# A short convolution of four taps spread over four 32-row tiles of the array, and a program put in line anew

## The chip, the cores and the metric

The kernel runs on one core of a Trainium2 chip. The metric is device time in microseconds (us) of one launch. Five engines work side by side and meet through semaphores: PE (TensorE, matmuls; its weight loads are listed apart as PEld), DVE (VectorE), ACT (ScalarE), POOL (GpSimd) and SP (SyncE), whose queue issues most of the transfers.

## The reference

All inputs are bf16. S = 2048 positions, D = 640 channels, F = 1728.

```python
x = A_q
h  = x + A(layernorm(x), k, v, shift_k, ssm_k, ssm_D)
h2 = h + B(layernorm(h))

def A(q, k, v, shift_k, ssm_k, ssm_D):
    # short causal convolution along the positions, each channel by itself
    k_pad = pad(k, 3 zero rows in front)
    k_shift = sum(k_pad[t:t + S, :] * shift_k[:, 3 - t] for t in range(4))
    kv = k_shift * v
    # long causal convolution of kv with ssm_k, by transforms over 2*S points
    y = irfft(rfft(pad(kv)) * rfft(pad(ssm_k)))[:S] + kv * ssm_D
    return q * y

def B(x):
    return (silu(x @ w_gate) * (x @ w_up)) @ w_down
```

## The kernel before

The 2048 positions go in four blocks of 512 (`BLK`); inside a block position 4p + r lies in partition p, row r (r = 0 to 3). For every block j the kernel

- loads k, turns it (channels to partitions) into `kT` and does the short convolution: for each r and each group c of 128 channels four matmuls add up in PSUM, with a slice of `kT` as weights and a 128x128 diagonal of tap weights (`diag`) streamed through. That is 4 x 5 x 4 = 80 pairs of weight load and matmul in a block (`kv_of`, line 540). The sum is multiplied by v into `kv` (tile t): in block 0 by DVE straight out of PSUM (line 545), in the others after a copy by ACT (line 547) by DVE (line 548), once for each r;
- transforms `kv` and the filter block `g` into spectra (`spectrum`, PE line 345, taken out of PSUM by ACT line 334 or DVE line 337), called X and G;
- multiplies and adds the spectra of all block pairs up to j on DVE (`mac`, lines 560, 582, 587, 588). Block 3 has the most of these;
- goes back by `inverse` (PE line 703), multiplies by the normed input, adds it to x (DVE lines 717, 723), norms the rows again and turns them into `hT` (`turn_h`, PE line 743 or a transposing transfer);
- runs the feed-forward part (`ffn`): gate and up products (PE lines 789 and 824), silu and product (ACT 807 and 813, DVE 815), down product with `wd` (PE line 856), output.

PSUM is eight banks, held as two pairs `ps_c` and two pairs `ps_f`. The conv side takes `ps_c` (in block 0 it takes `ps_f` and `ps_c` in turn, `conv_ps`), the feed-forward side takes `ps_f`.

The order of the work is made when the program is built. `Plan` holds every step with an engine, an assumed length, what it reads and writes and a priority; the priority of a stage is a due time plus the number that the table `PLACE` gives under the stage's name (Lk1 is the load of k of block 1, G2 the spectrum of filter block 2, m02 a product of spectra, i3 an inverse, f1 a feed-forward part). `schedule` then lists the steps one by one, and each engine gets its instructions in that order. So the table sets only the order in which instructions stand on each engine; on the chip each starts when those ahead of it on its engine are done and its semaphores are there.

The feed-forward part of block j stands beside the conv side of block j + 1, and that of block 3 stands alone at the end.

Of the kernel before, what the change touches and what calls it, by code (L numbers as in the profile page):

```python
# [11 lines left out]
BF16 = mybir.dt.bfloat16  # L12
# [14 lines left out]
KT = D // P  # L27
NC_FULL = 13
# [4 lines left out]
PAD = 16  # L33
DIRECT, ACTLN, ACTKV, ACTLN2 = ('inv0', 'G0', 'G1'), 1, 1, (2, 3)
# [5 lines left out]
PLACE = {"G0": 26.0, "G1": -15.5, "G2": -8.0, "G3": 12.0, "LWF": -13.5, "LWI": 16.0, "Ld": 20.0, "Lg0": -24.0,  # L40
# [47 lines left out]
class Plan:  # L88
# [4 lines left out]
    def __init__(self, slots, in_turn=()):  # L93
        self.ops, self.slots = [], slots
        self.turn = {t: [] for t in in_turn}
        self.at = {}
        self.all = 0.0

    def line(self, block, name, at, **own):

        at += PLACE.get(name, 0.0)
        self.block, self.all, self.at = block, at, {e: p + PLACE.get(name + e, 0.0) for e, p in own.items()}

    def add(self, eng, ns, fn, reads=(), writes=(), holds=(), other=None):
# [12 lines left out]
        op.other = other  # L117
        for acc, is_w in [(a, False) for a in reads] + [(a, True) for a in writes]:
            b, part = acc if isinstance(acc, tuple) else (acc, None)
            b.log.append((op, part, is_w))  # L120
# [5 lines left out]
    def schedule(self):  # L126
# [10 lines left out]
        while todo:  # L137
            found = []
            for op in todo:
                ready = 0.0  # L140
# [27 lines left out]
            assert best is not None, "the plan is stuck"  # L168
# [36 lines left out]
def kernel(ctx: ExitStack, tc: tile.TileContext, A_q, A_k, A_v, A_shift_k, A_ssm_k, A_ssm_D, B_x,  # L205
# [83 lines left out]
    diag = fixed([P, KT * 4, P], BF16, "diag")  # L289
# [212 lines left out]
    def load_k(j):  # L502

        kT = new("kT")
        if j == 0:
            load(MB, lambda: nc.sync.dma_start(out=plain(kT), in_=block(kk, j)), [kT])
        for r in range(R) if j else ():
            plan.add("turn", MB / 4 / 300.0, lambda r=r: nc.sync.dma_start(
                out=ap(kT)[:, :, r, PAD:], in_=block(kk, j)[:, r, :], transpose=True), [], [(kT, r)])
        return kT  # L510

    def turned_k(k):
        kT = new("kT")
        for r in range(R):
# [5 lines left out]
            pe(290, tr, [k, ident], [pt], [kT])  # L520
# [4 lines left out]
    def kv_of(j, kT, before, v):  # L525
# [7 lines left out]
        for r in range(R):  # L533
            ps = conv_ps()

            def mm(r=r, ps=ps):
                for c in range(KT):
                    for t in range(4):
                        q, off = (r - t, PAD) if r >= t else (r - t + 4, PAD - 1)
                        nc.tensor.matmul(line(ap(ps))[:, c * P:(c + 1) * P], ap(kT)[:, c, q, off:off + P],  # L540
                                         ap(diag)[:, 4 * c + t, :], start=(t == 0), stop=(t == 3))
            pe(1130, mm, [kT, diag], [ps], [kv])

            def straight(r=r, ps=ps):
                nc.vector.tensor_mul(ap(kv)[:, r, :], line(ap(ps)), rd(v)[:, r, :])
            if plan.block >= ACTKV:
                op = plan.add("act", 700, lambda r=r, ps=ps: nc.scalar.copy(ap(kv)[:, r, :], line(ap(ps))), [ps, v], [(kv, r)], (), ("dve", 820, straight))
                op.rest = dve(490, lambda r=r: nc.vector.tensor_mul(ap(kv)[:, r, :], ap(kv)[:, r, :], rd(v)[:, r, :]), [v], [(kv, r)])
            else:
                dve(820, straight, [ps, v], [(kv, r)])  # L550
        return kv

    def mac(A, X, H, first, pieces=((0, 1),), adds=()):
# [23 lines left out]
        for xs, hs, dst, f in ((0, 0, 0, nc.vector.tensor_add), (0, 1, 1, nc.vector.tensor_add),  # L577
# [3 lines left out]
            if (xs, hs) in adds:  # L581
                dve(1490, lambda b=b, xs=xs, hs=hs: nc.vector.tensor_mul(flat2(b), X.part(xs), H.part(hs)), [X.at(xs), H.at(hs)], [b], [A.b])
                add_into(lambda dst=dst: A.part(dst), lambda b=b: flat2(b), [b], [A.at(dst)])
                continue
# [164 lines left out]
    def load_w(gi):  # L749
        w = new("wgu")  # L750
        was = plan.all
        if plan.block == 0 and gi < 2:
            plan.all = PLACE.get("Lwg", 5.0)
        f0 = gi * 2 * P
# [10 lines left out]
        plan.all = was  # L765
# [116 lines left out]
    load(1e3, lambda: nc.sync.dma_start(out=ap(tapw), in_=A_shift_k.rearrange("(c p) t -> p c t", p=P)), [tapw])  # L882
# [3 lines left out]
    def blank():  # L886
# [3 lines left out]
    plan.add("pool", 2000, blank, [], [blanks])  # L890
    k = load_k(0)
    dve(2800, lambda: nc.vector.tensor_mul(
        ap(diag), ap(ident).unsqueeze(1).to_broadcast([P, KT * 4, P]),
        ap(tapw).rearrange("p c t -> p (c t)").unsqueeze(2).to_broadcast([P, KT * 4, P])), [ident, tapw], [diag])
# [130 lines left out]
```

## Time and profile before

| | us |
|---|---|
| median of 3 runs | 282.18 (281.87 to 284.87) |
| the profiled execution | 282.56 |
| its span, first to last instruction | 280.8 |
| PE busy | 260.9 (93%) |
| DVE busy | 207.0 (74%) |
| ACT busy | 175.6 (63%) |
| short convolution, PE matmuls of line 540 | 320 pairs |

Outside the span of the profiled execution lie 1.76 us. Busy times count each instruction from its start to its modelled end; matmuls overlap their neighbours, so what PE needs is read from how far apart starts lie, not from the mean length of one. The granted TensorE clock is 1.0 throughout.

### The profile page before, as it was taken

How to read it: one execution, taken by the hardware profiler on the slowest of the kernel's cores; microseconds unless marked ns; L12 is line 12 of the kernel's file. 1: busy time of each engine (PE TensorE's matmuls, PEld its weight loads, DVE VectorE, ACT ScalarE, POOL GpSimd, SP SyncE). 2: the span in 40 equal slices, each digit the busy share in tenths (PEclk: the TensorE clock that was granted, in tenths of full speed). 3: DMA queues.
4: the chain of work that ended last, by engine and by line, in shares of the span. 5: the costliest groups of instructions: out<-in, count | busy, mean ns of one | idle time of the engine just before them, and what ended most of it. 6: DMA issues, size and time to landing. Idle time of an engine off the chain costs nothing.

```text
span 280.8 us, 4663 instructions
## 1 busy us (share of the span) xinstructions
PE 260.9 (93%) x1787; PEld 162.0 (58%) x1804; DVE 207.0 (74%) x294; ACT 175.6 (63%) x285; POOL 52.8 (19%) x71
## 2 busy tenths in 40 slices
PE   0699989899999999999999999998989999999994
PEld 0686766645456677965545567643435774444672
DVE  0568996988999988899998999999999630011211
ACT  5547746998896877487756886386348643454300
POOL 2030100000398001131003101234950121000000
PEclk9999999999999999999999999999999999999999
DMA  7999992289957734959557495859545244653011
GB/s 251 338 366 237 240 233 98 93 194 250 258 118 92 216 122 101 170 83 205 143 141 150 98 245 85 174 117 232 148 102 152 27 47 86 170 154 59 0 49 48
DMA packets 74553, 42.77 MB, mean 152 GB/s; under 512 B 34145, under 2 KB 71842, under 8 KB 74530
## 3 DMA queue, kind: packets, MB, share of 16 engines
q1 hardware_dynamic: 71410, 37.88, 53.2%
q0 software_dynamic: 3120, 4.59, 11.6%
q8 instruction: 14, 0.23, 0.3%
q14 instruction: 9, 0.07, 0.1%
HBM read 30.01 MB, written 4.59 MB: 123 GB/s over the span
## 4 chain that ended last, share of the span: by engine, by line
PE 68%; DVE 16%; DMA 6%; ACT 6%; issue 2%; SPq 0%; DVEq 0%; ACTq 0%
PE ps_f L789 26%; PE ps_f L856 16%; PE ps_c L345 8%; PE ps_c L703 6%; DVE scr L587 5%; DVE S L588 5%; PE ps_c L540 5%; PE ps_f L824 4%; DMA kT<-in_A_k_dram 2%; DMA ld<-in_A_ssm_k_dram 2%; DMA wgu<-in_B_w_gate_dram 2%; ACT S L334 2%; DVE S L560 1%; PE ps_f L540 1%; ACT sg L807 1%
## 5 line engine op out<-in xcount | busy, mean ns | idle before, releaser
L789 PE MATMUL ps_f<-hT,wgu 128*128 128x512 bf16 x465 | 106.6, 379 | 3.3 <-ACT sg L807 2.3
L789 PEld LDWEIGHTS <-wgu 128*128 128x128 bf16 x480 | 46.7, 98 | 56.2 <-issue 2.8
L856 PE MATMUL ps_f<-wd,tT 128*128 128x320 bf16 x448 | 63.5, 299 | 0.1
L856 PEld LDWEIGHTS <-tT 128*128 128x128 bf16 x448 | 43.7, 98 | 17.2 <-issue 0.4
L807 ACT ACTIVATE sg<-ps_f 128x1024 bf16<-128x1024 f32 (+1 forms) x28 | 27.0, 963 | 24.6 <-PE ps_f L789 12.5
L815 DVE TENSOR_TENSOR tT<-sg,sg 128x1024 bf16<-128x1024 bf16 (+1 forms) x27 | 17.5, 647 | 27.4 <-ACT sg L813 27.4
L345 PE MATMUL ps_c<-t,WF 128*128 128x320 bf16 x208 | 34.9, 299 | 0.6 <-ACT S L334 0.5
L813 ACT CAST sg<-ps_f 128x1024 bf16<-128x1024 f32 (+1 forms) x27 | 25.6, 950 | 14.5 <-PE ps_f L789 14.5
L588 DVE TENSOR_TENSOR S<-S,scr 128x2560 bf16<-128x2560 bf16 x21 | 31.4, 1493 | 0.7
L587 DVE TENSOR_TENSOR scr<-S,S 128x2560 bf16<-128x2560 bf16 x21 | 31.2, 1485 | 0.3 <-DMA S<-scr 0.2
L345 PEld LDWEIGHTS <-WF 128*128 128x128 bf16 x240 | 23.4, 98 | 13.2 <-issue 1.5
L598 ACT ACTIVATE row<-x 128x640 bf16<-128x640 bf16 x32 | 23.4, 733 | 5.5 <-DVE x L723 5.1
L862 POOL DMA_DIRECT2D out_dram<-o x12 | 10.6, 883 | 70.7 <-ACT o L861 70.7
L334 ACT CAST S<-ps_c 128x640 bf16<-128x640 f32 (+1 forms) x31 | 18.9, 622 | 7.0 <-PE ps_c L345 6.4
L540 PEld LDWEIGHTS <-kT 128*128 128x128 bf16 x320 | 20.1, 103 | 2.3 <-issue 0.8
L540 PE MATMUL ps_c<-diag,kT 128*128 128x128 bf16 x280 | 17.7, 223 | 0.7 <-DVE hT L745 0.7
L648 ACT ACTIVATE row<-x,sm 128x640 bf16<-128x640 bf16 x17 | 15.0, 919 | 2.7 <-DMA x<-row 1.3
L637 ACT ACTIVATE row<-x 128x640 bf16<-128x640 bf16 x16 | 11.7, 731 | 7.5 <-DMA x<-in_A_q_dram 7.5
L703 PEld LDWEIGHTS <-WI 128*128 128x128 bf16 x128 | 12.4, 98 | 6.8 <-issue 1.2
L861 ACT CAST o<-ps_f 128x640 bf16<-128x640 f32 x12 | 8.2, 687 | 10.8 <-PE ps_f L856 10.8
L717 DVE SCALAR_TENSOR_TENSOR row<-row,ps_c 128x640 bf16<-128x640 bf16 x14 | 11.5, 819 | 3.7 <-PE ps_c L703 3.6
L824 PE MATMUL ps_f<-hT,wgu 128*128 128x512 bf16 x58 | 13.8, 379 | 0.1
(105 smaller groups left out, 293.6 us busy)
## 6 DMA issues: line engine op xcount, KB each, us to landing
wgu<-in_B_w_gate_dram SPq DMA_DIRECT2D x24, 320.0 KB, 3.5
wgu<-in_B_w_up_dram SPq DMA_DIRECT2D x24, 320.0 KB, 3.6
x<-in_A_q_dram SPq DMA_DIRECT2D x4, 640.0 KB, 3.8
ld<-in_A_v_dram SPq DMA_DIRECT2D x4, 640.0 KB, 5.8
ld<-in_A_ssm_k_dram SPq DMA_DIRECT2D x4, 640.0 KB, 5.3
wd<-in_B_w_down_dram SPq DMA_DIRECT2D x1, 2080.0 KB, 12.0
out_dram<-x SPq DMA_DIRECT2D x3, 640.0 KB, 3.6
out_dram<-o POOLq DMA_DIRECT2D x12, 160.0 KB, 3.5
```

The lines of the kernel that those rows point to most:

```text
L334: (lambda: nc.scalar.activation(dst(), src(), ACT.Copy, scale=2.0)) if twice else (lambda: nc.scalar.copy(dst(), src())),
L345: nc.tensor.matmul(ap(ps)[:, h, 0:NH], w, ap(src)[:, r, h * NH:(h + 1) * NH], start=(first and i == 0), stop=(last and i == len(rs) - 1), ...
L540: nc.tensor.matmul(line(ap(ps))[:, c * P:(c + 1) * P], ap(kT)[:, c, q, off:off + P], ap(diag)[:, 4 * c + t, :], start=(t == 0), stop=(t == 3))
L587: nc.vector.tensor_mul(flat2(b), X.part(xs), H.part(hs))
L588: f(A.part(dst), A.part(dst), flat2(b))
L598: act(930, lambda r=r, junk=junk: nc.scalar.activation(ap(junk), ap(x)[:, r, :], ACT.Square, scale=D ** -0.5, accum_out=sm(s, 1)[:, r:r + ...
L703: nc.tensor.matmul(ap(ps)[:, w, 0:NH], m, src[:, w * NH:(w + 1) * NH], start=(i == 0), stop=(i == len(terms) - 1))
L789: nc.tensor.matmul(of(ps, i), ap(w)[:, k, off:off + P], ap(hT)[:, k, lo:lo + n], start=(k == 0), stop=(k == KT - 1))
L807: act(1010 if wide else 600, lambda: nc.scalar.activation(of(sg), of(*gate), ACT.Silu), [(gate[0], gate[1] + i) for i in range(m)], [sg])
L813: op = plan.add("act", 1010 if wide else 590, lambda: nc.scalar.copy(of(co), of(*up)), psu + [sg], [co] + tt, (), ("dve", 1230 if wide els ...
L824: nc.tensor.matmul(ap(ps)[:, i, :], ap(w)[:, k, off:off + P], ap(hT)[:, k, :], start=(k == 0), stop=(k == KT - 1))
L856: nc.tensor.matmul(ap(ps)[:, hf, 0:NH], ap(tT)[:, c, at:at + P], ap(wd)[:, c, hf * NH:(hf + 1) * NH], start=(c == order[0]), stop=(c == or ...
```

## The change

It does four things.

1. The short convolution runs on four tiles of 32 rows of the array. A tile b holds 32 of the 128 channels of a group; its sums go to a PSUM bank of its own, so a step holds two pairs (four banks) at once. For each group of channels there are seven runs per tile, over 128, 96, 64, 32, 32, 64 and 96 columns, which write several r at once; that is 28 pairs of weight load and matmul for a group. A block has one step of four groups (112 pairs) and one of a single group (28 pairs). `diag` shrinks from 128 to 32 columns and is made from a small `eye`. The sums come out by bank: two ACT copies (or DVE products in block 0) of 128x512 for each pair and one of 128x256 for the last group, and for blocks 1 to 3 one DVE product over the whole block takes the place of four.
2. k of block 0 is loaded in two halves, ahead of most else, and its turning waits half by half; 24 matmuls on the identity (`warm`) stand first on PE.
3. Loads are given earliest times (`HOLD`), which the scheduler respects when it lists them. The chip does not see these times, only the order.
4. All numbers of `PLACE` are new, and a product that is added by a transfer is now listed behind the writers of what it is added to.

```diff
+ROWT = P // 4
+WARM = 24
-PLACE = {"G0": 26.0, "G1": -15.5, ... }
+PLACE = {"G0": 16.6, "G1": 8.7, ... }
+HOLD = {"LWF": 4000, "LWI": 18000, "Lg1": 22000, ... }
...
-                ready = 0.0
+                ready = op.hold
...
-    diag = fixed([P, KT * 4, P], BF16, "diag")
+    diag = fixed([P, KT * 4, ROWT], BF16, "diag")
+    eye = fixed([P, 2 * ROWT], BF16, "eye")
...
-            load(MB, lambda: nc.sync.dma_start(out=plain(kT), in_=block(kk, j)), [kT])
+            for lo in (0, 2):
+                load(MB // 2, lambda lo=lo: nc.sync.dma_start(out=plain(kT)[:, lo:lo + 2], in_=block(kk, j)[:, lo:lo + 2, :]), [(kT, ("in", lo // 2))])
...
-        for r in range(R):
-            ps = conv_ps()
...
-                        nc.tensor.matmul(line(ap(ps))[:, c * P:(c + 1) * P], ap(kT)[:, c, q, off:off + P],
-                                         ap(diag)[:, 4 * c + t, :], start=(t == 0), stop=(t == 3))
-            pe(1130, mm, [kT, diag], [ps], [kv])
...
-                op = plan.add("act", 700, lambda r=r, ps=ps: nc.scalar.copy(ap(kv)[:, r, :], line(ap(ps))), [ps, v], [(kv, r)], (), ("dve", 820, straight))
-                op.rest = dve(490, lambda r=r: nc.vector.tensor_mul(ap(kv)[:, r, :], ap(kv)[:, r, :], rd(v)[:, r, :]), [v], [(kv, r)])
...
+            runs = [(q, PAD, q, R, 0) for q in range(R)] + [(q, PAD - 1, 0, q, R - q) for q in range(1, R)]
+            for i, c in enumerate(cs):
+                for n, (q, off, lo, hi, t) in enumerate(runs):
+                    for b in range(R):
+                        ch = slice(b * ROWT, (b + 1) * ROWT)
+                        nc.tensor.matmul(ap(banks[b // 2])[:, b % 2, (i * R + lo) * ROWT:(i * R + hi) * ROWT], ap(kT)[ch, c, q, off:off + P],
+                                         ap(diag)[ch, R * c + t:R * c + t + hi - lo, :], start=(n == 0), stop=(n == len(runs) - 1),
+                                         tile_position=(b * ROWT, 0), skip_group_check=True)
...
+        for cs in (range(4), range(4, KT)):
+            banks = (conv_ps(), conv_ps())
+            pe(250 * len(cs) + 200, lambda cs=cs, banks=banks: taps(cs, banks), [kT, diag], list(banks), [kv])
...
+                        act(600 if len(cs) > 1 else 400, lambda to=to, src=src: nc.scalar.copy(to(ap(kv)), src()), [ps, v], [(kv, (len(cs), i, h)) if plan.block >= ACTKV else kv])
+                        dve(690 if len(cs) > 1 else 420, lambda to=to, src=src: nc.vector.tensor_mul(to(ap(kv)), src(), to(rd(v))), [ps, v], [(kv, (len(cs), i, h)) if plan.block >= ACTKV else kv])
+        if plan.block >= ACTKV:
+            dve(1490, lambda: nc.vector.tensor_mul(ap(kv), ap(kv), rd(v)), [v], [kv])
...
+    def warm():
+        for _ in range(WARM):
+            nc.tensor.matmul(ap(idle)[:, 0, 0:P], ap(ident), ap(ident), start=True, stop=True)
```

How the instructions stand at three places. First SP's queue, the first transfers of the program. x_76 is the block of A_q, kT_80 the k of block 0 as it is loaded, tapw the tap weights, ld_77 v, ld_78 the filter block, WF the forward basis. Before:

```order
L312 DMA x_76<-in_A_q_dram 128x2560
L900 DMA WF<-const_wf 128x2048
L882 DMA tapw<-in_A_shift_k_dram 128x5x4
L506 DMA kT_80<-in_A_k_dram 128x2560
L307 DMA ld_77<-in_A_v_dram 128x2560
L300 DMA ld_78<-in_A_ssm_k_dram 128x5x512
L763 DMA wgu_85<-in_B_w_gate_dram 128x5x256
```

And of the change:

```order
L322 DMA x_76<-in_A_q_dram 128x2560
L517 DMA kT_80<-in_A_k_dram 128x1280
L919 DMA tapw<-in_A_shift_k_dram 128x5x4
L517 DMA kT_80<-in_A_k_dram 128x1280
L949 DMA row_87<-in_A_ssm_D_dram 1x640
L317 DMA ld_77<-in_A_v_dram 128x2560
L310 DMA ld_78<-in_A_ssm_k_dram 128x5x512
L789 DMA wgu_85<-in_B_w_gate_dram 128x5x256
L940 DMA WF<-const_wf 128x2048
```

WF has gone from ahead of k to behind v, the filter block and a first feed-forward weight. Further on, `wd` (2.1 MB), which stood right behind `const_minus`, now stands far behind, after the filter block, k and v of blocks 1 and 2 and the weights of the first six feed-forward groups of block 0.

Second, the start of DVE's queue, up to the first sum taken of block 0's spectrum (the tile scr_72 of line 337, line 347 in the change); t_81 is `kv`, t_82 the turned filter block. Before:

```order
L892 TENSOR_TENSOR diag<-ident,tapw 128x2560
L521 COPY kT_79<-ps_c_94 128x5x128
L521 COPY kT_79<-ps_c_95 128x5x128
L545 TENSOR_TENSOR t_81<-ps_f_96,ld_77 128x640
L545 TENSOR_TENSOR t_81<-ps_c_94,ld_77 128x640
L430 COPY t_82<-ps_c_95 128x640
L430 COPY t_82<-ps_c_94 128x640
L545 TENSOR_TENSOR t_81<-ps_f_97,ld_77 128x640
L545 TENSOR_TENSOR t_81<-ps_c_95,ld_77 128x640
L337 TENSOR_SCALAR scr_72<-ps_f_97 128x320
```

And of the change:

```order
L932 TENSOR_TENSOR diag<-eye,tapw 128x640
L532 COPY kT_79<-ps_f_97 128x5x128
L532 COPY kT_79<-ps_c_94 128x5x128
L532 COPY kT_79<-ps_f_96 128x5x128
L532 COPY kT_79<-ps_c_95 128x5x128
L573 TENSOR_TENSOR t_81<-ps_f_97,ld_77 128x4x4x32 x2
L573 TENSOR_TENSOR t_81<-ps_c_94,ld_77 128x4x4x32 x2
L573 TENSOR_TENSOR t_81<-ps_f_96,ld_77 128x2x4x32
L573 TENSOR_TENSOR t_81<-ps_c_95,ld_77 128x2x4x32
L442 TENSOR_TENSOR t_82<-t_82,row_87 1x640
L440 COPY t_82<-ps_f_97 128x640
L440 COPY t_82<-ps_c_95 128x640
```

All four copies of the turned k are now DVE's (ACT did two), the products with v come by bank instead of by row, and the copies of the turned filter block stand behind them.

Third, PE at the short convolution of block 1, which in both programs stands behind the spectra of block 0 and ahead of block 0's inverse. Before, one of the 40 pairs that stand here (the others of block 1 stand later in two lots of 20):

```order
L540 LDWEIGHTS kT_80
L540 MATMUL ps_c_94<-diag,kT_80 128x128
```

And of the change, the first of 112 pairs:

```order
L551 LDWEIGHTS kT_80
L551 MATMUL ps_c_94<-diag,kT_80 128x128
L551 LDWEIGHTS kT_80
L551 MATMUL ps_c_94<-diag,kT_80 128x128
L551 LDWEIGHTS kT_80
L551 MATMUL ps_c_95<-diag,kT_80 128x128
L551 LDWEIGHTS kT_80
L551 MATMUL ps_c_95<-diag,kT_80 128x128
L551 LDWEIGHTS kT_80
L551 MATMUL ps_c_94<-diag,kT_80 128x96
L551 LDWEIGHTS kT_80
L551 MATMUL ps_c_94<-diag,kT_80 128x96
```

Four pairs that follow each other go to the four tiles, two banks of ps_c_94 and two of ps_c_95; then the next run of columns follows. Both pairs of `ps_c` are held until ACT has copied them.

More of the change, by code (lines that the diff above doesn't have):

```diff
@@ L96, in __init__ @@
         self.at = {}
-        self.all = 0.0
+        self.all = self.hold = 0.0
     def line(self, block, name, at, **own):
         at += PLACE.get(name, 0.0)
-        self.block, self.all, self.at = block, at, {e: p + PLACE.get(name + e, 0.0) for e, p in own.items()}
+        self.hold = HOLD.get(name, 0.0)
+        self.block, self.all = block, at
+        self.at = {e: own.get(e, at) + PLACE.get(name + e, 0.0) for e in ("pe", "act", "dve")}
     def add(self, eng, ns, fn, reads=(), writes=(), holds=(), other=None):
@@ L117, in add @@
         op.other = other
+        op.hold = self.hold if eng in self.ISSUE else 0.0
         for acc, is_w in [(a, False) for a in reads] + [(a, True) for a in writes]:
@@ L167, in schedule @@
                            key=lambda f: (f[0][1] // 5, f[0][0], f[0]))
-            assert best is not None, "the plan is stuck"
+            assert best is not None, f"the plan is stuck at {len(order)}"
             (start, _, _), op, way = best
@@ L532, in kv_of, with taps @@
         kv = new("t4")
-        for r in range(R):
-            ps = conv_ps()
[L536 to L540, printed above, removed]
-                                         ap(diag)[:, 4 * c + t, :], start=(t == 0), stop=(t == 3))
-            pe(1130, mm, [kT, diag], [ps], [kv])
[L544 to L550, printed above, removed]
+        def taps(cs, banks):
+            runs = [(q, PAD, q, R, 0) for q in range(R)] + [(q, PAD - 1, 0, q, R - q) for q in range(1, R)]
[6 more added lines that the diff above has]
+                                         tile_position=(b * ROWT, 0), skip_group_check=True)
@@ L764, in load_w @@
                 out=ap(w)[:, :, to:to + n], in_=cols(src, lo, n)), [(w, i)])
-        plan.all = was
+        plan.all, plan.hold = was
         return w
@@ L890, with fold @@
     plan.add("pool", 2000, blank, [], [blanks])
+    first("Lk0", 0.01)
     k = load_k(0)
-    dve(2800, lambda: nc.vector.tensor_mul(
-        ap(diag), ap(ident).unsqueeze(1).to_broadcast([P, KT * 4, P]),
-        ap(tapw).rearrange("p c t -> p (c t)").unsqueeze(2).to_broadcast([P, KT * 4, P])), [ident, tapw], [diag])
+    first("Lt", 0.02)
+    load(1e3, lambda: nc.sync.dma_start(out=ap(tapw), in_=A_shift_k.rearrange("(c p) t -> p c t", p=P)), [tapw])
+    first("warm", 0.0)
+    idle = new("ps_f")
+    def warm():
+        for _ in range(WARM):
+            nc.tensor.matmul(ap(idle)[:, 0, 0:P], ap(ident), ap(ident), start=True, stop=True)
+    pe(110 * WARM, warm, [ident], [idle])
+    first("diag", 0.0)
+    def fold():
+        nc.vector.tensor_add(ap(eye), ap(ident)[:, 0:2 * ROWT], ap(ident)[:, 2 * ROWT:P])
+        nc.vector.tensor_add(ap(eye)[:, 0:ROWT], ap(eye)[:, 0:ROWT], ap(eye)[:, ROWT:2 * ROWT])
+    dve(300, fold, [ident], [eye])
+    dve(820, lambda: nc.vector.tensor_mul(
+        ap(diag), ap(eye)[:, 0:ROWT].unsqueeze(1).to_broadcast([P, KT * 4, ROWT]),
+        ap(tapw).rearrange("p c t -> p (c t)").unsqueeze(2).to_broadcast([P, KT * 4, ROWT])), [eye, tapw], [diag])
     first("Lx0", 0.1)
```

27 lines of the change are left out of this document (22 added, 5 removed), and 16 rows, old and new, of the table PLACE.

## The prediction

> **What bounds the kernel now.** I read the page first, then the chain that ended last, then the waits of each engine, then single rows.
>
> ```profile
> PE 260.9 (93%) x1787; PEld 162.0 (58%) x1804; DVE 207.0 (74%) x294; ACT 175.6 (63%) x285; POOL 52.8 (19%) x71
> PE   0699989899999999999999999998989999999994
> DVE  0568996988999988899998999999999630011211
> PE 68%; DVE 16%; DMA 6%; ACT 6%; issue 2%; SPq 0%; DVEq 0%; ACTq 0%
> ```
>
> Two engines are near full at once. DVE stands mostly at 8 or 9 tenths from the fourth slice to the thirty-first (21 to 218 us) and then has little to do; PE is full throughout. A saving on one of them alone need not reach the end. The chain, in pieces:
>
> ```profile
> 2.19 6.55 DMA kT<-in_A_k_dram
> 11.69 2.21 PE ps_f L540 x19
> 19.19 0.84 DVE t L545
> 27.03 5.88 DMA ld<-in_A_ssm_k_dram
> 32.98 2.56 ACT scr L415
> 36.18 1.25 PE ps_c L703 x8
> 112.63 4.47 PE ps_c L540 x80
> ...
> 204.34 0.61 DVE tT L815
> 205.04 1.03 ACT sg L807
> 212.75 0.54 PE ps_c L703 x4
> 232.72 10.74 PE ps_f L789 x49
> 261.67 15.39 PE ps_f L856 x112
> ```
>
> Three stretches can be seen. Up to 36 us it is a start that only waits: k lands, is turned, goes through the taps, DVE multiplies, the spectra follow. From 36 to 212 PE and DVE share it. At 212.75 the inverse of block 3 begins; what follows is PE alone: 280.8 - 212.75 = 68.05 us of products, the same instructions before and after. So the end moves as the start of this inverse moves. Who holds that point is told by two rows.
>
> ```profile
> 211.46 0.82 DVE L681 TENSOR_TENSOR S<-S 128x1280 bf16<-128x1280 bf16 x1
> 212.59 0.71 PE L703 MATMUL ps_c<-S,WI 128*128 128x320 bf16 x4
> ```
>
> L681 makes the input of the first L703 and is done at 212.28; PE gets to L703 at 212.59. Both arrive together: DVE is as much the bound of this point as PE. That decides the sum: **the end can come no earlier than DVE's stream lets it**, whatever PE saves.
>
> **What the taps cost on PE.** Before, 80 pairs take 4.47 us in the chain, 56 ns a pair. A pair of 512 columns takes 10.74 / 49 = 219 ns and one of 320 takes 15.39 / 112 = 137 ns, so a column is worth (219 - 137) / 192 = 0.43 ns. After, a group of 128 channels has 28 pairs, but each of the four tiles streams only 128 + 96 + 64 + 32 + 32 + 64 + 96 = 512 columns. The trace has no tiled matmul, so I bound it. Best: the four tiles run wholly side by side, 0.219 us a group, 1.1 us a block. Worst: nothing overlaps and each pair goes at today's pace although it has fewer columns: 140 x 56 ns = 7.8 us a block. On top comes going from the whole array to tiles and back.
>
> ```profile
> L540 PE MATMUL ps_c<-diag,kT x280: 216/219/311, 13.7 to 116.9; 128*128 128x128 bf16 x140
> ```
>
> A matmul lasts 219 ns where the next starts after 56, so emptying the array costs at most 0.16 us; four changes a block make 0.65. I take 1.1 + 0.65 = **1.75 us a block**, near the lower end, since the diff gives each tile array rows and a bank of its own, so that neither an input nor a result of one is another's; blocks 1 to 3 then save 3 x (4.47 - 1.75) = 8.2 us of PE.
>
> The Trainium skill speaks against this: TensorE: Matmul & The Clock Gate, section LDWEIGHTS, says that a load's time goes with its columns and that a load of 32 rows takes as long as one of 128. By that alone the 140 loads would cost like 140 of today's, the worst end. The same page, section The mechanism, says that loads and matmuls of different row groups overlap, which gives the best end. No row here can tell.
>
> **The start.** Rows in order:
>
> ```profile
> 1.97 0.29 POOL L884 TENSOR_SCALAR_AFFINE_SELECT ident<-ident 128x128 bf16<-128x128 bf16 x1
> 4.29 0.74 ACT L637 ACTIVATE row<-x 128x640 bf16<-128x640 bf16 x1 [2.22 <-DMA x<-in_A_q_dram]
> 7.23 2.83 DVE L892 TENSOR_TENSOR diag<-ident,tapw 128x2560 bf16<-128x2560 bf16 x1 [6.10 <-DMA tapw<-in_A_shift_k_dram]
> 8.79 0.71 PE L519 MATMUL ps_f<-ident,kT 128*128 128x128 bf16 x5 [8.79 <-DMA kT<-in_A_k_dram]
> 13.69 1.87 PE L540 MATMUL ps_c<-diag,kT 128*128 128x128 bf16 x20
> 16.34 1.11 DVE L430 COPY t<-ps_c 128x640 bf16<-128x640 bf16 x2
> 20.01 0.49 DVE L337 TENSOR_SCALAR scr<-ps_f 128x320 bf16<-128x320 f32 x1
> ```
>
> x is there at 4.2 and k at 8.7; WF (0.52 MB) and k (0.66 MB) came between, 0.26 MB a us. Without WF the two halves of k land at about 5.5 and 6.8. The tap weights, behind x and half of k, land near 6.4; `diag` has a quarter of its columns, 0.7 us, done by 7.2. DVE then makes the four copies of kT (0.49, then 0.41 each when they follow closely, 1.7 in all): taps can begin at **9.0 instead of 11.7**. The clock: the first 19 taps took 2.21 us, twice the later pace, and the full pace came within the group of 20 that began at 13.69, some 6 us after PE's first matmul at 8.79. With the 24 warming matmuls from 2.3 us on (ident is ready then) the same 6 us end at 8.4, so I take the taps of block 0 as fast. Four groups and a change: 1.1 us, to 10.1. Then DVE: four products of 128x512, which I put at 0.69 between the 0.49 of 320 and the 0.82 of 640 columns, and two of 0.42: 3.6 us, to 13.7. Two copies (1.11) now stand behind them: 14.9 for the first sum of the spectrum, where 20.01 stood. **Gain 5.1 us**. WF, needed at 13.7, now stands behind 2.9 MB: at the 0.26 MB a us of above it lands at 15, at the page's rates of the first two slices at 12.
>
> ```profile
> GB/s 251 338 366 237 240 233 98 93 194 250 258 118 92 216 122 101 170 83 205 143 141 150 98 245 85 174 117 232 148 102 152 27 47 86 170 154 59 0 49 48
> ```
>
> (1.8 MB by 7.0, then 0.34 a us.) I take it as in time, since the transfers behind k run in those faster slices; late, it costs up to 1.3. So the gain's ends are 0, where something else in the start is late (rival two), and 6.2, where the two copies find a gap.
>
> By the Trainium skill (TensorE: Matmul & The Clock Gate, What's actually happening) the clock rises after some 3.4 us of sustained matmuls; 24 at half pace last 2.6 us, so by that rule warming would fall short and the taps of block 0 take 1 us longer. The 6 us in this trace fit a window that must be full.
>
> **DVE from there to the inverse of block 3.** Its instructions are the same but for three kinds.
>
> ```profile
> L548 DVE TENSOR_TENSOR t<-t,ld 128x640 bf16<-128x640 bf16 x12 | 5.5, 486 | 0.9 <-ACT t L547 0.9
> L588 DVE TENSOR_TENSOR S<-S,scr 128x2560 bf16<-128x2560 bf16 x21 | 31.4, 1493 | 0.7
> L337 DVE CAST scr<-ps_c 128x640 bf16<-128x640 f32 x1 | 0.8, 824 | 0.2 <-ACT row L637 0.2
> ```
>
> Twelve products of 486 become three of 1.49: -1.3 us. One eviction of 128x640 more goes to DVE: +0.8. **-0.5 us.** What remains is DVE's waiting:
>
> ```profile
> DVE row L717 <- PE ps_c L703: 3.2, 7, 0.8
> DVE S L397 <- ACT S L334: 1.0, 1, 1.0
> DVE t L548 <- ACT t L547: 0.9, 2, 0.6
> DVE sm L605 <- ACT row L598: 0.9, 1, 0.9
> DVE S L337 <- PE ps_f L345: 0.9, 2, 0.5
> ```
>
> Between 20 and 215 us its waits add up to 10.4 us, of which these are the largest. Most wait for PE, or for ACT behind PE. With PE 8 us lighter some of them go: in block 0's inverse, for one, 20 taps (1.12 us) no longer stand between L703's parts, where DVE waited 0.8. But new ones come: the product over a whole block waits for the last of six ACT copies, and a step of taps needs both `ps_c` pairs empty, so that the matmuls behind it on PE stand still until ACT has copied. I take **-2.5 us**, with -8 (nearly all go) and +3 (one full wait of 0.5 us for each of the six steps) as ends. ACT's copies cost 12 x 0.59 + 6 x 0.4 = 9.5 us instead of 8.1, on an engine busy for 63%.
>
> The load of `wd` leaves the start and stands in front of block 0's last weights; it may hold PE for a us or two near 85 us, which I put at nothing, since PE then has about 5 us of slack against DVE.
>
> **Sum.** On the profiled execution: span 280.8 - 5.1 (start) - 0.5 (work) - 2.5 (waits) = 272.7; with 1.76 outside the span 274.5. That execution (282.56) stands 0.4 above the median, so against the median **274.1 us**, 2.9% faster. PE for its part could end at 280.8 - 5.1 - 8.2 = 267.5: it is not the bound, by 5 us.
>
> **Rivals.**
> *One: tiles do not overlap.* Each block then takes 7.8 us: 3 x 3.3 = 10.0 us more on PE in blocks 1 to 3, and block 0's 112 pairs take 6.3 instead of 1.1, which eats the gain of the start. PE sets the end: 280.8 + 10.0 + 1.8 - 0.4 = 292.2, **slower**. For it: loads are 140 instead of 80, and no row shows two matmuls at once. Against it: each tile has rows and a bank of its own. It decides from here: PE's 267.5 rises by 3.8 blocks x the excess, and passes 280.8 where a block takes 1.75 + 13.3 / 3.8 = 5.25 us, 37 ns a pair.
> *Two: the start is given back.* The chain at 27.03 goes through the filter block of block 1: landed at 32.9, copied by ACT for 2.56, and the tap copies stand behind it on ACT, the inverse behind those. That load must follow block 0's transfers on SP. In the change it stands behind four transposing loads and WI; if these are no quicker, 36.18 stays and only 0.5 + 2.5 are won: 279.2. For it: SP has more in front; against: `wd` (2.1 MB) is out of the way.
> *Three: PE's saving shows in full.* DVE's waits nearly vanish, and the end is PE's: 267.5 + 1.8 - 0.4 = 268.9.
>
> **Chances.** Forecast 0.57 (its own range, from the ends of start and waits, 269 to 279.5), rival one 0.12, two 0.16, three 0.12, 0.03 for something slower still unnamed. The range 268 to 284 takes in those ends and leaves out rival one, the unnamed and a little of three. About 1% (2.8 us) is what a measurement of this kernel can tell from no change; under 279.4 fall the forecast, rival three and over a third of rival two: faster 0.75, same 0.12, slower 0.13.
>
> **What would show it.** Taps: a block's 140 pairs within 2.5 us of PE. Start: first taps near 9, DVE's first spectrum sum near 15, inverse of block 0 near 31 instead of 36. Bound: the first L703 of block 3's inverse near 204.7, with DVE's last input just before it and PE idle ahead of it. I am wrong if the taps run over 37 ns a pair, or if the filter block of block 1 lands near 33 again.

## The result, and the profile after

The changed kernel takes **272.08 us** (median of 4 runs, 271.44 to 273.11) where the kernel before, run beside it on the same chip, took 283.52 (median of its three runs above and a fourth): a ratio of 0.960 (0.9522 to 0.9678). Run again on another chip it took 271.94 where the kernel before took 283.62: 0.9592 (0.9558 to 0.9626). So it is 4% faster; 274.1 was forecast.

The page of the changed kernel: busy time of each engine, the slices of PE and DVE, the granted clock, and the engines' shares of the chain that ended last.

```profile
PE 253.5 (94%) x2052; PEld 151.1 (56%) x2068; DVE 205.4 (76%) x292; ACT 173.7 (64%) x288; POOL 53.5 (20%) x71
PE   5699998999999999999999999999899999999993
DVE  1787998999999999999989989999998511212221
PEclk9689999999999999999999999999999999999998
PE 62%; DVE 24%; ACT 7%; issue 4%; DMA 2%; SPq 0%; DVEq 0%; ACTq 0%
```

PE lost 7.4 us of work, DVE 1.6. Two landmarks cut both executions into three stretches: the first matmul of block 0's inverse and the first of block 3's. The windows between them, of the kernel before (columns: window, length, busy us of PE, PEld, DVE, ACT, POOL with instructions in brackets, clock, DMA share, GB/s):

```profile
32.97:212.59 179.62, 173.45 (x1154) 104.45 (x1166) 167.18 (x217) 129.48 (x203) 43.72 (x44) 1.00 0.71 157
212.59:280.80 68.21, 64.22 (x398) 38.21 (x399) 20.38 (x49) 26.82 (x38) 3.49 (x4) 1.00 0.34 78
```

and of the changed kernel:

```profile
28.53:200.96 172.43, 167.14 (x1266) 95.89 (x1273) 166.42 (x209) 127.93 (x208) 45.18 (x44) 1.00 0.74 172
200.96:269.70 68.74, 64.25 (x398) 38.21 (x399) 20.78 (x49) 26.40 (x37) 3.48 (x4) 0.99 0.33 77
```

| us | before | after | difference |
|---|---|---|---|
| start, up to block 0's inverse | 32.97 | 28.53 | -4.4 |
| middle, up to block 3's inverse | 179.62 | 172.43 | -7.2 |
| end | 68.21 | 68.74 | +0.5 |
| PE idle in the middle (length less busy) | 6.2 | 5.3 | -0.9 |
| DVE idle in the middle | 12.4 | 6.0 | -6.4 |

The start gave about what was forecast; the middle gave more than twice the 3.0 us forecast for it. Its last column says how: PE's idle time hardly changed, so the middle shrank by PE's work (6.3 us less), and DVE, whose work fell by 0.8, simply stood less. One thing to keep in mind for later: block 1's first step of taps stands ahead of block 0's inverse, and so in the start; there it has 112 pairs now, where 40 stood before.

The taps, from the chain of the changed kernel (block 2) and from its list for line 551:

```profile
111.39 1.11 PE ps_c L551 x112
127.88 0.36 PE ps_c L551 x28
```

```profile
L551 PEld LDWEIGHTS <-kT x560: 90/93/142, 8.2 to 128.0; 32*128 32x128 bf16 x187
```

140 pairs take 1.11 + 0.36 = 1.47 us, 10 ns a pair, where 80 took 4.47. Each load still lasts 93 ns, as long as a load of 128 rows did (98): the Trainium skill (TensorE: Matmul & The Clock Gate, LDWEIGHTS) says so, and the trace agrees. But they overlap, as the same page (The mechanism) has it for different row groups: loads of 93 ns start every 10 ns.

Block 3's inverse in the changed kernel, PE and DVE by time:

```profile
198.81 2.32 PE L850 MATMUL ps_f<-hT,wgu 128*128 128x512 bf16 x10
200.96 0.71 PE L728 MATMUL ps_c<-S,WI 128*128 128x320 bf16 x4
199.81 0.82 DVE L706 TENSOR_TENSOR S<-S 128x1280 bf16<-128x1280 bf16 x1
```

Once more both arrive together: DVE is done at 200.63, PE comes straight from line 850 at 200.96, with no idle time ahead, where the prediction had PE idle. From 61 to 90 us and from 158 to 193, though, the chain that ended last runs mostly through DVE's products of spectra. It comes back to PE through ACT, for which PE has waited; PE has four such waits (line 815 for ACT's line 833), 2.2 us in all. One of them:

```profile
178.77 0.61 DVE tT L841
179.46 1.03 ACT sg L833
180.54 2.53 PE ps_f L815 x11
```

So the two engines lie close together, and neither the chain nor the last handover says what a lighter or a heavier one would cost. That has to be tried.

### The profile page after: what moved, and what is told of

Its sections match the earlier page's. It is cut to its first block, busy times and chain, and to the rows that moved or that the text cites. A ratio compares the mean times of both kernels' runs of the same rounds, so it can differ in the third digit from the quotient of the medians.

```text
span 269.7 us, 5199 instructions
## 1 busy us (share of the span) xinstructions
PE 253.5 (94%) x2052; PEld 151.1 (56%) x2068; DVE 205.4 (76%) x292; ACT 173.7 (64%) x288; POOL 53.5 (20%) x71
## 4 chain that ended last, share of the span: by engine, by line
PE 62%; DVE 24%; ACT 7%; issue 4%; DMA 2%; SPq 0%; DVEq 0%; ACTq 0%
PE ps_f L815 24%; PE ps_f L882 16%; PE ps_c L355 8%; DVE S L613 7%; DVE scr L612 6%; PE ps_c L728 4%; PE ps_f L850 3%; PE ps_f L355 2%; DMA tapw<-in_A_shift_k_dram 2%; PE ps_f L728 2%; ACT S L344 2%; ACT sg L833 2%; DVE tT L841 2%; DVE row L742 1%; PE ps_c L551 1%
## 5 line engine op out<-in xcount | busy, mean ns | idle before, releaser
L344 ACT CAST S<-ps_c 128x640 bf16<-128x640 f32 (+1 forms) x28 | 17.0, 630 | 5.6 <-PE ps_c L355 5.2
L585 DVE TENSOR_TENSOR S<-S,S 128x2560 bf16<-128x2560 bf16 (+1 forms) x10 | 12.0, 1218 | 0.1
L344 ACT ACTIVATE scr<-ps_c 128x640 bf16<-128x640 f32 (+1 forms) x17 | 11.3, 692 | 1.1 <-PE ps_c L355 1.1
```

What stands on the lines that cost most here:

```text
L344: (lambda: nc.scalar.activation(dst(), src(), ACT.Copy, scale=2.0)) if twice else (lambda: nc.scalar.copy(dst(), src())),
```

## The experiments

All start from the changed kernel; its median is 272.0 (272.08 and 271.94). The third column takes the difference of medians, the last that of the ratios to the kernel before run beside each, times 282.8, about what the kernel before takes. The runs were on four chips, on which the kernel before took 282.6 to 283.6; where the two columns differ, the last is to be gone by.

| run | median us | to 272.0 | ratio to before | by the ratios |
|---|---|---|---|---|
| changed kernel again | 271.94 | - | 0.9592 (0.9558-0.9626) | - |
| taps twice, blocks 1-3 | 290.18 | +18.2 | 1.0228 (1.0166-1.0291) | +18.0 |
| taps three times | 298.7 | +26.7 | 1.0552 (1.0504-1.06) | +27.1 |
| two DVE products fewer | 272.27 | +0.3 | 0.9608 (0.956-0.9657) | +0.5 |
| old table | 317.82 | +45.8 | 1.1215 (1.1161-1.1269) | +45.9 |
| taps tile by tile | 278.46 | +6.5 | 0.9838 (0.9795-0.9882) | +7.0 |
| 5.2 us more PE | 275.59 | +3.6 | 0.9756 (0.9703-0.9809) | +4.6 |
| whole-array taps, blocks 1-3 | 277.68 | +5.7 | 0.983 (0.9776-0.9885) | +6.7 |
| warm-up between the turns | 274.81 | +2.8 | 0.9721 (0.968-0.9762) | +3.6 |
| one warm-up matmul | 274.65 | +2.7 | 0.9678 (0.9641-0.9716) | +2.4 |
| tap weights in ACT's queue | 271.24 | -0.8 | 0.9558 (0.9526-0.9591) | -1.0 |
| that, and PE kept at work | 274.22 | +2.2 | 0.9679 (0.9642-0.9715) | +2.5 |

### Which engine holds the middle

**DVE lighter.** Two of block 3's products of spectra (6.0 us of DVE) are left out.

```diff
-            dve(2980, go, [X.at(xs), H.at(hs)], [b, A.at(dst)])
+            skip = plan.block == 3 and X is Xs.get(3) and xs == 0
+            dve(2980, None if skip else go, [X.at(xs), H.at(hs)], [b, A.at(dst)])
```

> The changed kernel without two of the four products of block 3's own spectra (X3 with H0): two pairs of multiply and add on DVE, 4 x 1.49 = 6.0 us of DVE less between 184 and 200 us, left out of the result. Theory A (DVE holds the inverse of block 3): the inverse starts some 5 us sooner, time near 267. Rival B (PE holds it): at most 1 us sooner, 271 to 272.

Measured 272.27: nothing gained. In the trace the middle lasts 171.5 instead of 172.4; DVE's idle time in it rose from 6.0 to 10.2, PE's fell from 5.3 to 4.5. The row of DVE's waits in the middle that grew, here and in the changed kernel:

```profile
DVE tT L844 <- ACT sg L842: 5.5, 6, 2.1
```

```profile
DVE tT L841 <- ACT sg L839: 1.3, 3, 0.5
```

DVE now waits for ACT's copies of PE's up products: the time it was spared became a wait behind PE, and from 183 us on the chain of this run is PE's. That holds for the products that were left out, the last ones. The earlier ones still stand in the chain (64 to 86 and 161 to 181 us), and no run made those lighter or heavier.

**PE heavier, evenly.** 24 of the gate and up groups of blocks 0 and 1 get one matmul more.

```diff
-                    for k in range(KT):
+                    for extra in ((0, 1) if j < 2 and i % 2 == 0 else (1,)):
+                        nc.tensor.matmul(of(ps, i), ap(w)[:, 0, off:off + P], ap(hT)[:, 0, lo:lo + n], start=True, stop=(extra == 0))
+                    for k in range(1, KT):
```

> 24 more matmuls of 128x512, spread one by one over the gate and up groups of blocks 0 and 1 (the first of five weights is multiplied twice, the first product being written over), 24 x 0.216 = 5.2 us of PE, all ahead of block 3's inverse, order kept, no burst. Theory A of the prediction (DVE's stream sets block 3's inverse, PE has about 5 us of slack there): 272-273. Theory B (PE's stream sets it): the whole 5.2 us, 277.3 from 272.1, and first inverse matmul of block 3 at 206.2 instead of 200.96.

```profile
31.36:207.39 176.03, 171.90 (x1289) 98.32 (x1297) 167.20 (x210) 128.47 (x208) 43.64 (x44) 1.00 0.73 167
```

The middle is 3.6 us longer for 5.2 us of work, the median 3.6 (4.6 by the ratios); PE's idle time in it fell from 5.3 to 4.1. So PE's slack was 0.6 to 1.6 us, not 5: theory A falls, and theory B is nearly right. All of this work stands ahead of 160 us, so it says nothing of the last stretch in which the chain goes through DVE.

**Whole-array taps in blocks 1 to 3, order kept.** POOL builds the wide diagonal early (5.1 us).

```diff
+        def whole(cs, banks):
+            for r in range(R):
+                for i, c in enumerate(cs):
+                    for t in range(4):
+                        q, off = (r - t, PAD) if r >= t else (r - t + 4, PAD - 1)
+                        nc.tensor.matmul(ap(banks[r // 2])[:, r % 2, i * P:(i + 1) * P], ap(kT)[:, c, q, off:off + P],
+                                         ap(wide_diag)[:, 4 * c + t, :], start=(t == 0), stop=(t == 3))
...
+                        if not b0:
+                            return ap(ps)[:, h[0], :] if len(cs) > 1 else ap(ps)[:, :, 0:P]
```

> The changed kernel in its own order, but the taps of blocks 1 to 3 run on the whole array as before (80 matmuls of 128x128 a block on a wide diagonal that POOL builds early, 4.47 us a block for 1.47), with as many copies of the same sizes. PE gains 3 x 3.0 = 9.0 us of work ahead of block 3's inverse. Theory B (PE's stream sets it): 272.1 + 9.0 = 281. Theory A (5 us of slack): 276. Third theory (what the kernel gained after the start comes from the order alone): 272-273.

5.7 us (6.7 by the ratios) of the 9.0 show. So the tiles in blocks 1 to 3 are worth 6 to 7 us of the whole time, and the third theory, that the order alone brings what was gained after the start, falls. The middle of this run:

```profile
29.80:206.68 176.88, 173.07 (x1132) 103.08 (x1141) 165.35 (x207) 126.69 (x207) 42.18 (x44) 1.00 0.72 166
```

It is 4.4 us longer than the changed kernel's and 2.7 shorter than that of the kernel before; the start, in which block 1's first step of taps stands, is 1.3 longer. So the tiles bring some 4.4 of the 7.2 us of the middle. (In five more profiles whose edit leaves the middle alone it takes 172.55 to 173.60, so this can be 1 us less.) The other 2.7 no run parts: the new order has its share, and so has block 1's step, of which 64 pairs of the whole array stand ahead of the middle here, where the kernel before had 40.

**Tile by tile.** The same 28 matmuls of a group, but seven on one tile, then seven on the next.

```diff
-                for n, (q, off, lo, hi, t) in enumerate(runs):
-                    for b in range(R):
+                for b in range(R):
+                    for n, (q, off, lo, hi, t) in enumerate(runs):
```

> The 28 tap matmuls of a group are issued tile by tile (seven on the first 32 rows, then seven on the next, and so on) and no longer in turn over the four tiles; number, sizes and sums are the same, and so is every order between groups. Theory 'the tiles run side by side': neighbours now lie on the same rows and take turns, so a group of 28 goes from 0.277 us to 28 x 37 ns = 1.04 us or more, a block's five from 1.47 to 5.2 us or more, blocks 1 to 3 by 11 us; with PE as the bound the median goes from 272.1 to 281-285, with PE 5 us off the bound to 277-280. Rival 'the small matmuls are short by themselves, in any order': 0.277 us a group stays and the time is 272.

The chain has

```profile
116.91 2.53 PE ps_c L551 x97
134.76 0.79 PE ps_c L551 x25
```

The chain counts only the matmuls that it passes; the list of PE by time has all 112 of the first step:

```profile
116.84 2.60 PE L551 MATMUL ps_c<-diag,kT 32*128 32x128 bf16 x112
```

So 112 pairs take 2.53 us and 28 take 0.79, that is 23 and 28 ns a pair instead of 10, and 3.3 us a block for 1.47. That is less than the 37 ns I expected, but the theory stands: neighbours on one tile take turns, neighbours on four do not. A tile also has a PSUM bank of its own, so this run does not tell whether it is the rows of the array or the bank that neighbours must not share. Four blocks get 4 x 1.85 = 7.4 us more PE, of which 6.5 to 7.0 show.

**Taps twice, and three times.** In blocks 1 to 3 all tap matmuls are issued again into the same banks. These were the first tries at loading PE.

```diff
-            pe(250 * len(cs) + 200, lambda cs=cs, banks=banks: taps(cs, banks), [kT, diag], list(banks), [kv])
+            def run(cs=cs, banks=banks, n=2 if plan.block else 1):
+                for _ in range(n):
+                    taps(cs, banks)
+            pe(250 * len(cs) + 200, run, [kT, diag], list(banks), [kv])
```

> The changed kernel, in which blocks 1 to 3 run their 140 pairs of taps twice (the second pass writes the same sums again); the order of everything is kept. A block's taps took 1.11 + 0.36 = 1.47 us of PE in the changed kernel's trace, so PE gets 4.4 us more. Theory A, the prediction's: DVE holds the start of block 3's inverse and PE has some 5 us of slack there, so the time rises by 1.5 us at most (272.1 to 273.6) and the inverse stays near 201 us. Rival B: PE holds it (the tiles only freed DVE from waiting for PE): the time rises by the full 4.4, to 276.5, and the inverse starts near 205.4.

> The same with three passes: 4.4 us a block, what the whole-array taps took before (4.47), with the order of the change. 8.8 us more PE. Theory A: the first 5 us are hidden, the rest shows, about 276. Rival B: all shows, 280.9. If B holds, this run also says what the tiles are worth by themselves in blocks 1 to 3.

Both theories missed by far: 4.4 us of matmuls cost 18, 8.8 cost 27. The chain of the first of the two:

```profile
69.90 2.27 PE ps_c L551 x217
72.17 2.73 issue
...
123.35 1.61 PE ps_c L551 x167
124.96 4.80 issue
```

The pace is as before (224 pairs, of which the chain counts 217, in 2.27 us: 10 ns a pair), but behind it PE stands for 2.7 and 4.8 us with "issue", that is, waiting for nothing that the profile shows. The rows of such waits before the taps' loads (total, times, longest), in the changed kernel and in the one with taps three times:

```profile
PEld L551 <- issue: 2.7, 7, 0.5
```

```profile
PEld L551 <- issue: 15.8, 12, 3.0
```

The stalls of over 2 us, three with taps twice and five with three times, come behind 128 to 224 of these pairs in a row; in the changed kernel, with 112 in a row, there are only the seven waits of at most 0.5 us. What PE lacks is its next instructions, by the transfers in the trace. Queue q8 carries instructions in pieces of 16 KB, and its row on the three pages (changed kernel, taps twice, three times; pieces, MB, share) grows with PE's loads and matmuls (4120, 4959, 5799), while DVE, ACT and POOL have as many instructions as before:

```profile
q8 instruction: 16, 0.26, 0.4%
q8 instruction: 19, 0.31, 0.5%
q8 instruction: 23, 0.38, 0.5%
```

In each of the eight stalls one such piece is on its way, and PE goes on 1.3 to 1.8 us after it has landed: in the stall at 72.17 the piece moves from 72.3 to 73.4, and PE's next load starts at 74.7. This is read from the traces; no run tested it by itself.

With taps twice the three stalls add up to 10.1 us and the work to 4.4, so some 3.5 of the 18 are left. These are likely pace: in or behind each stall the granted clock (third number from the end) falls to half for 3.4 to 6.8 us.

```profile
75.60:79.00 3.40, 3.40 (x10) 1.21 (x9) 1.81 (x2) 2.85 (x7) 0.31 (x1) 0.50 0.42 111
```

So these two runs say nothing on slack, and the even dose above took their place.

### The order

**The old table.** The changed kernel with `PLACE` as it was and no `HOLD`.

```diff
-PLACE = {"G0": 16.6, "G1": 8.7, "G2": -3.8, "G3": 32.1, "LWF": 2.4, ...}
-HOLD = {"LWF": 4000, "LWI": 18000, ...}
+PLACE = {"G0": 26.0, "G1": -15.5, "G2": -8.0, "G3": 12.0, "LWF": -13.5, ...}
+HOLD = {}
```

> The changed kernel with the table of numbers of before and without earliest times: tiles, folded diag, halved k and warming matmuls stay, the order of the loads and of the stages is nearly that of before (WF ahead of k again, wd early again). Theory A: the tiles and the lighter PE carry most of the gain, and the old order loses mainly the start, 2 to 4 us: 274 to 277. Rival C: the new order carries the gain: 279 or more.

46 us more. The longest of PE's waits, and SP's rows at its place in the program:

```profile
PEld L812 <- DMA x<-in_A_q_dram: 23.2, 1, 23.2
```

```profile
204.73 5.47 SPq L758 DMA_TRANSPOSE hT<-row  x3
210.31 1.27 SPq L319 DMA_DIRECT2D x<-in_A_q_dram  x1
```

The load of x stands behind the turning of h on SP and is issued at 210; PE has nothing for 23 us. Another 11 us go at 31 us, at block 1's taps:

```profile
PE ps_c L548 <- ACT t L568: 11.5, 2, 10.8
```

ACT's copies out of `ps_c` stand there behind its copy of a filter block that lands at 38 us, much as in rival two of the prediction. The numbers of a table fit the pieces that they were made for; the run says nothing on what the new order is worth with the new pieces. By the run with whole-array taps some 2.7 of the middle's 7.2 us are left for the order and the rest there; what it brought at the start can't be parted from the loads it moved.

### The start

**One warm-up matmul for 24.**

```diff
-        for _ in range(WARM):
+        for _ in range(1):
```

> One warm-up matmul in place of 24, all else in order. Theory 'they are worth what the slow turns cost': the turns of k at 0.5 us for 0.29, two of them on the way to the taps, which run at half clock either way: 0.2 to 0.5 us, median 272.3-272.6. Rival 'the warm-up keeps the clock up for the whole of block 0's start': 1.5 us or more, 273.5.

2.4 to 2.7 us, so the rival is nearer. Without the warm-up the turns of k, the taps (0.43 us a group), the turns of g and the first steps of the spectrum run at half pace. Two rows of PE in this run, and one of the changed kernel run again, where the full pace came:

```profile
18.52 0.74 PE L355 MATMUL ps_c<-t,WF 128*128 128x320 bf16 x2
19.53 0.43 PE L355 MATMUL ps_c<-t,WF 128*128 128x320 bf16 x2
```

```profile
16.53 0.43 PE L355 MATMUL ps_f<-t,WF 128*128 128x320 bf16 x2
```

The full pace comes 3 us later, up to 1.1 of it by the landing of the tap weights (7.25 for 6.18), which differs from execution to execution, see below. And 24 matmuls do not always do it. The run with two DVE products fewer has them too, but in its profile five turns of k's second half take 0.5 us, half the pace, and the full pace first comes at 18.6 us; with taps twice it first comes at 17.6.

```profile
9.35 0.71 PE L530 MATMUL ps_f<-ident,kT 128*128 128x128 bf16 x5 [2.61 <-DMA kT<-in_A_k_dram]
```

**Warm-up between the turns.** 20 matmuls of ident by ident behind k's second quarter.

```diff
                     nc.tensor.transpose(turned(pt)[:, c * P:(c + 1) * P], plain(k)[:, r, c * P:(c + 1) * P], ap(ident))
+                for _ in range(20 if r == 1 else 0):
+                    nc.tensor.matmul(ap(pt)[:, 1, 0:P], ap(ident), ap(ident), start=True, stop=True)
```

> 20 more matmuls of ident by ident between the turns of k's second and third quarter of rows, where PE waits for k's second half, so that PE's clock is up when block 0's taps begin. Theory 'the taps of block 0 are slow (0.427 us a group for 0.277) because the clock had fallen in the wait': about 4 x 0.15 = 0.6 us less before the first sum on DVE and 0.3 to 1 us more in the turns of g and the first spectrum: 271.0-271.7. Theory 'the start is set by the copies and products of ACT and DVE': no change, 272, or +0.5 if the added work delays the turn.

The taps did go at full pace (0.25 us a group), yet the run is 3 us slower, which neither theory allows.

```profile
6.50 2.02 PE L532 MATMUL ps_c<-ident 128*128 128x128 bf16 x20
9.16 0.45 PE L530 MATMUL ps_f<-ident,kT 128*128 128x128 bf16 x5 [0.65 <-DMA kT<-in_A_k_dram]
16.20 0.27 PE L438 MATMUL ps_c<-ident,ld 128*128 128x128 bf16 x1 [0.42 <-issue]
```

The 20 ran at half pace until 8.5. In the two profiles of the changed kernel the turn behind them began at 7.2 to 7.5, so there they would have stood in its way by 1 us or so. In this execution they did not: the turn still waited 0.65 us for k's second half, which came late (9.16), behind the tap weights (8.34). A stall of 0.42 without a named cause follows at 16.2. The first inverse began at 30.48 instead of 28.53, most of that with the late landing. All six runs are slower (274.2 to 276.5), so there is a cost; what makes it stays open.

**The changed kernel again**, unaltered, beside the next run.

> The changed kernel unaltered, beside the next two on one chip. Both theories: 272.1 as before, between 271 and 273; its first tap weights (tapw) may land anywhere from 5.9 to 8.6 us, as in the eight profiles with this order of loads, and block 0 moves with them.

271.94, as before. Its tap weights landed early, `diag` beginning at 6.18 us.

**The tap weights in ACT's queue.** In the ten profiles with the new order of loads the product `diag` began, with the landing of the tap weights, anywhere between 5.89 and 8.56 us (ten kernels with the same loads up to there), and the turn of k's second half 0.8 to 1.2 us behind it each time.

```diff
-    load(1e3, lambda: nc.sync.dma_start(out=ap(tapw), ...), [tapw])
+    tap_load = load(1e3, lambda: nc.scalar.dma_start(out=ap(tapw), ...), [tapw])
...
+        line_up.remove(tap_load)
+        line_up.insert(0, tap_load)
```

> The 5 KB of tap weights (640 rows of 8 bytes) are issued by ACT's own queue as the first thing, no longer by SP between the two halves of k; all else in order. Theory 'tapw holds the start': in eight profiles it landed 4.1 to 6.8 us after its issue and k's second half 0.4 to 1.3 us behind it, so out of that queue it lands near 5 at the latest, k's second half at about 6.5 instead of 7.1-9.4, the first spectrum sum on DVE near 15 instead of 16.0 (17 to 18 in the slower profiles), and the median falls by 1 to 2 us, to 270-271. Rival 'k's second half is late from its own bytes and the queue's load': no change, 272.

```profile
4.90 0.82 DVE L932 TENSOR_TENSOR diag<-eye,tapw 128x640 bf16<-128x640 bf16 x1 [2.21 <-DMA tapw<-in_A_shift_k_dram]
6.95 0.45 PE L530 MATMUL ps_f<-ident,kT 128*128 128x128 bf16 x5 [0.40 <-DMA kT<-in_A_k_dram]
```

The weights land at 4.9 and k's second half at 6.95, earlier than in any profile with the old queue, and the median is 0.7 us (1.0 by the ratios) lower than that of the changed kernel beside it. The intervals of the two ratios overlap, so this is likely, not shown.

**PE kept at work as well.** In the changed kernel run again the pace falls back to half at 13 us, behind two waits of 1.1 and 0.8 us, and stays there for 3 us (in its first profile it fell at 8.8, behind a wait of 1.25, for 7 us). So the two waits were filled with 24 and 12 matmuls.

```diff
+            for _ in range(24 if j == 0 and cs[0] == 4 else 0):
+                nc.tensor.matmul(ap(banks[1])[:, 1, 2 * P:3 * P], ap(ident), ap(ident), start=True, stop=True)
...
+                for _ in range(12 if r == 0 and drow is not None else 0):
+                    nc.tensor.matmul(ap(pt)[:, 1, 2 * P:3 * P], ap(ident), ap(ident), start=True, stop=True)
```

> As the run with the tap weights in ACT's queue (271.24), and PE is kept at work in the two waits that came before its clock fell in block 0: 24 matmuls of ident by ident behind the last taps (1.3 us for a wait of 1.15) and 12 behind the first turn of g (0.66 for 0.76), into parts of PSUM nobody reads. Theory 'the idle time lets the clock fall': the turns of g stay at 0.28 us for five and the first spectrum's pairs at 0.27 us for 0.53; some 8 pairs and 3 turns are slow now, 2.8 us of PE, half or more of it before DVE's first sums: 1 to 2 us less, 269.2-270.2. Rival 'the clock falls by itself some 7 us after it rose, whatever PE does': pairs at 0.53 as before, 271.2-272.

```profile
12.14 0.72 PE L440 MATMUL ps_f<-ident 128*128 128x128 bf16 x10
15.49 0.27 PE L440 MATMUL ps_f<-ident 128*128 128x128 bf16 x2 [2.62 <-issue]
17.56 0.74 PE L355 MATMUL ps_f<-t,WF 128*128 128x320 bf16 x2
```

Amid the filling PE stalls for 2.62 us on "issue", as with the doubled taps, and as there a 16 KB piece of instructions is on its way (12.8 to 14.0 us): 140 tap pairs, 24 filling ones, a turn of 5 and 10 more of filling had gone since 8.34 us. The stall is longer than the waits that were to be filled, the pace falls behind it all the same, and the run is 3.0 us (3.4 by the ratios) slower than with the tap weights in ACT's queue alone. Whether the idle time lets the pace fall stays open, since no run kept PE at work there. The profiles speak for it: in seven the granted clock rose at 5.3 to 6.4 us; it fell 3.4 us later in the four in which PE waited 1.25 to 2.5 us for k's second half, and 6.8 us later in the three in which it waited 0.4 to 0.8.

## Why the prediction was right, and where it was wrong

The number came out 2.0 us above the measured one, and the direction is right, but that it is so near is partly luck: the middle was taken 4.2 us too small, for a wrong reason, and start and end went the other way.

- **The bound: wrong step.** "DVE is as much the bound of this point as PE", and so "the end can come no earlier than DVE's stream lets it", with 5 us of slack for PE. The last handover showed both arriving together, but in the middle as a whole DVE stood idle for 12.4 us and PE for 6.2. Taking 6.0 us from DVE's last products gained nothing; giving PE 5.2 and 9.0 us cost 3.6 to 4.6 and 5.7 to 6.7. PE's slack is 0.6 to 3.3 us. These are runs of the changed kernel, and DVE's earlier products were not tried. The two rows of the last handover were also read too evenly: from 206.5 us to the inverse the chain of the kernel before is PE's alone, with 0.05 us of idle time, and DVE was done 0.3 us ahead of PE. The piece of that chain in front of the inverse:

```profile
210.59 2.16 PE ps_f L824 x10
```

- **DVE's waits: the term that was too small.** -2.5 us was taken, with ends of -8 and +3; DVE's idle time in the middle fell by 6.4. It is the same mistake: DVE waited for PE, directly or through ACT, and waits less when PE has less to do. Rival three, "PE's saving shows in full" (268.9), had the better mechanism, though its time is 3.2 us off: 0.6 to 0.9 of PE's time shows.
- **DVE's work: right.** -0.5 forecast, -0.8 measured.
- **The taps: right.** 1.75 us a block forecast, 1.47 measured; that is 0.37 above the bound of 1.1. Of the 0.65 us for going between array and tiles the rows show a part: behind three of the six steps of blocks 1 to 3 PE stands for 0.16 us, which is the size that was reckoned for one change, and behind whole-array taps it does not.

```profile
82.02 1.03 PE L815 MATMUL ps_f<-hT,wgu 128*128 128x512 bf16 x4 [0.16 <-issue]
```

  Rival one (37 ns a pair) is out: 10 ns as built, and even one tile after another 23 to 28.
- **The start: nearly right.** Forecast -5.1, inverse of block 0 near 31 instead of 36; by the matmul that starts it on `ps_c` it began at 30.78 for 36.18 (-5.4), by its first one -4.4. On the way to it two steps missed and one was lucky:

```profile
6.48 0.82 DVE L932 TENSOR_TENSOR diag<-eye,tapw 128x640 bf16<-128x640 bf16 x1 [3.79 <-DMA tapw<-in_A_shift_k_dram]
7.50 0.45 PE L530 MATMUL ps_f<-ident,kT 128*128 128x128 bf16 x5 [1.25 <-DMA kT<-in_A_k_dram]
16.02 0.95 DVE L347 TENSOR_SCALAR scr<-ps_c 128x320 bf16<-128x320 f32 x2 [0.54 <-ACT scr L344]
```

  The tap weights landed at 6.4 as reckoned, but k's second half at 7.5, not 6.8. The taps ran from 8.16 to 10.97, at half pace (0.43 us a group), where I took them as fast; in the execution of the kernel run again they took 0.25. DVE's first sum stood at 16.02, not 14.9. What made up for it is the stretch behind: the filter block of block 1 was issued at 20.73 instead of 27.03, so rival two did not come about.
- **The clock: wrong reading.** I read 6 us of work from the trace before. The first turn of k was fast at 5.5 us in the profiled run, 3.2 us after the first warm-up matmul, and at 6.1 in another, 3.8 after it. That is near the 3.4 us of the Trainium skill (TensorE: Matmul & The Clock Gate, What's actually happening). My use of it, that 24 matmuls fall short, did not hold there, as the turns follow close enough; it did hold in two other profiles (first full pace at 17.6 and 18.6 us). That the pace falls back behind waits of about 1 us I had not reckoned with; in the profiled run it fell at 8.8, ahead of most of block 0's taps.
- **`wd` later: right.** PE has no wait for it in the middle.
- **The end: small miss.** The last stretch was taken as fixed; it is 0.5 us longer.

Summed: 280.8 - 4.4 - 7.2 + 0.5 = 269.7, against a forecast of 272.7. The start was reckoned 0.7 us too good and the end 0.5 too short; the miss is the middle, 4.2 us more than its two terms, nearly all of it in DVE's waits (-6.4 for -2.5).

## What to carry to other kernels

Where two engines arrive together at the point that sets the end, these two rows do not say which of them holds it. Add up the idle time of each over the whole stretch before it; here the fuller engine (6.2 us idle against 12.4) was the better guess. Then try it, by a little more work for one engine and a little less for the other: after the change the two idle times were nearly alike (5.3 and 6.0 us), and only the runs told that PE's work still shows, by 0.6 to 0.9. A table of the order belongs to the pieces that it was made for: under the old table the new pieces lost 46 us, while under the new one whole-array taps in blocks 1 to 3 lost 6 to 7.

## What was not expected of the hardware

- PE runs dry behind long rows of small pairs: eight stalls of 2.2 to 4.8 us on "issue" behind 128 to 224 tap pairs at 10 ns, and one of 2.62 us amid 36 filling matmuls behind the taps, each with a 16 KB piece of instructions on its way. So matmuls that seemed free for lying in a wait cost more here than the wait.
- A transfer of 5 KB in 640 pieces of 8 bytes, between two halves of k, landed 4.1 to 6.8 us after its issue in ten executions, and k's second half came behind it each time. The product `diag`, for which block 0 waits, began up to 2.7 us earlier or later by that.
- In the two profiles of the changed kernel the pace of matmuls fell to half with no wait over 1.3 us before it. The granted clock of the profile does not always show the half pace: in the run with one warm-up matmul the clock column of the windows (the third from the end) says 1.00 while each pair of 320 columns took 0.27 us, twice what it takes later. The trace of that run has no record of the clock ahead of 19.5 us, where the full pace begins, and the column says 1.00 for what is not recorded. The 1.0 throughout of the kernel before is to be read in the same way: its first 19 taps went at half pace.

```profile
14.00:17.00 3.00, 2.70 (x20) 2.24 (x20) 2.27 (x6) 1.58 (x3) 0.05 (x1) 1.00 1.37 196
17.00:20.00 3.00, 3.00 (x15) 1.78 (x14) 1.48 (x3) 1.19 (x4) 0.00 (x0) 1.00 1.04 298
```
